# Half of a DFT's tables made on GpSimd instead of loaded, and another order of DMAs at the seam to the next stage

## The chip, the cores and the metric

One core of a Trainium2 chip runs the whole program. The metric is the device time in microseconds (us) of one execution; a lower one is better. The engines are TensorE (PE, with its weight loads PEld), VectorE (DVE), ScalarE (ACT), GpSimd (POOL) and SyncE (SP), and 16 DMA engines that all queues share. "SPq" and "ACTq" rows are DMA issues in the queues of SyncE and ScalarE.

## The reference, cut to what matters

A long convolution by FFT, gated by x, and behind it two dense layers:

```
h = (relu(pos_emb @ w1) @ w2) * exp(-0.01 * pos)      # 12480 x 128
u = x * v                                             # 2 x 12480 x 128
y = irfft(rfft(u, 2S) * rfft(h, 2S))[:S]
z = x * y
z = relu(z @ w_in)**2 @ w_out                         # 128 -> 2048 -> 128
z = (g * cos(g)) @ w_out2, g = z @ w_in2              # 128 -> 2048 -> 128
```

## The kernel before

The FFT is split as 104 x 120, and the program has three stages. **Stage 1** runs over 30 chunks q (`NCH`), each of two pairs i of sequence offsets (`CB`). `load(q)` brings one row block per chunk, `ld[q]`: 128 partitions x 2672 floats, holding x, v, a table `et` of cosines and sines (416 floats, `2 * KR`) and the position embedding. `mlp1` and `prep` make h (two matmuls, ACT) and u = x * v (GpSimd) in the tile `ut`; `pair(q, i)` multiplies u and h by the table on TensorE (`A`), ACT copies one half of the result to `v`, DVE writes sum and difference to the tile `bt`, and `store(q)` sends `bt` to the DRAM array `Bs`. The second pair of a chunk uses the same table with its halves swapped, and chunk 0 has one more table, in the tile `first` together with the small weights.

The chunks go through five load slots (`LDB`), so `load(q)` waits in SP's queue until PE is done with chunk q - 5. `prep` runs up to five pairs (`LA`) ahead of `pair`, and a tile `ut` comes free when `pair` of chunk q - 3 is done. Between pairs, `decode(2)` advances the unpacking of the 16 weight parts of the dense layers: seven steps to a part, so one part every 3.5 pairs, with five tensor_scalar (L101, L102, L104, L106, L109) and two two-input operations (L107, L112) on DVE and two (L114, L116) on GpSimd; L114 waits for L112's result. Each engine runs its instructions in the order in which the code is written (`manual_schedule`).

**Stage 2** multiplies along the other axis. `load2(g)` brings `B2[g]` from `Bs`, 26 groups of 8 rows, into the ring slots that chunks 25, 26 and 27 had; H, Z and d are its matmuls. At **the seam** the newest chunks are not yet in `Bs`. For chunks q >= `LATE` = 28 the first 32 rows (`KE`) go to a small DRAM array `Bx` by `store_late(q)` instead; `Bs` has zeros at their places; and `load_late(g)` then copies them into `B2[g]`, behind `load2(g)`. For group 0 the last chunk skips DRAM: four `direct` copies go from `bt` to `B2[0]`. `load2(0)` reads `Bs` and so waits for the landing of the store of chunk LATE - 1, which is issued at pair (LATE, 0). The stores of chunks 28 and 29 proper stand in SP's queue. **Stage 3**, the dense layers, takes the rest and isn't touched.

Of the kernel before, what the change touches and what calls it, by code (L numbers as in the profile page):

```python
# [8 lines left out]
F32 = mybir.dt.float32  # L9
# [4 lines left out]
ALU = mybir.AluOpType  # L14
# [23 lines left out]
LA = LDB = 5  # L38
NB = 3
BT = 3  # L40
LATE = NCH - 2
KE = 32
FIRST = 384 + 4 * NCH + 2 * KR
XVE, SLOT = 2048 + 2 * KR, 3072
CROSS = (1, 1)
WS = 59
INV2PI = 0.15915494309189535
# [9 lines left out]
def conv_moe(ctx, tc, t):  # L57
    nc = tc.nc
# [79 lines left out]

    def load_late(g, n=CB * (NCH - LATE)):

        for r in range(2):
            a = HB * r + CB * LATE
            nc.sync.dma_start(out=B2[g][a:a + n].rearrange("p k c e -> p k (c e)"),
                              in_=Bx[2 * G4 * g + r:2 * G4 * (g + 1):2, 0:n].rearrange("k p e -> p k e"))


    with ExitStack() as st:
        out1 = st.enter_context(tc.tile_pool(name="out1", bufs=BT))
        c1 = st.enter_context(tc.tile_pool(name="c1", bufs=1))
        ring1 = st.enter_context(tc.tile_pool(name="ring1", bufs=LDB - NB, side="right"))  # L150
        io = st.enter_context(tc.tile_pool(name="io1", bufs=2))
# [4 lines left out]
        first = c1.tile([128, FIRST], F32, name="first")  # L156
        w1b, w2b = first[:, 0:128], first[:, 128:384]
        win = first[0:N1, 384:384 + 4 * NCH].rearrange("p (q i a) -> p q i a", q=NCH, i=CB)
        emid = first[0:N1, 384 + 4 * NCH:FIRST].rearrange("p (a m) -> p a m", a=2)
        ld = {}  # L160

        def load(q):
            sl = slot("ld", *((ring, SLOT) if q % LDB < NB else (ring1, XVE + CB * N1)))
            nc.sync.dma_start(out=sl[:, 0:XVE + CB * N1], in_=t["ld"][q])
            x, v = (sl[0:N1, 1024 * n:1024 * (n + 1)].rearrange("p (i a d) -> p i a d", i=CB, a=2) for n in range(2))
            et = sl[0:N1, 2048:XVE].rearrange("p (a m) -> p a m", a=2)
            pt = sl[:, XVE:XVE + CB * N1].rearrange("p (i k) -> p i k", i=CB)
# [10 lines left out]
        def mlp1(q):  # L178
# [4 lines left out]
            nc.scalar.activation(hT, hp, AF.Relu)  # L183
            hT_t[q] = hT

        def prep(q, i):
            _, xt, vt, _ = ld[q]
            if i == 0:
                ut_t[q] = io.tile([N1, CB, 2, 384], F32, tag="ut", name="ut", bufs=3)
            u = ut_t[q]  # L190
            nc.gpsimd.tensor_tensor(out=u[:, i, :, 0:256], in0=xt[:, i], in1=vt[:, i], op=ALU.mult)
            hp = psM.tile([128, 2 * D], F32, tag="m", name="hp2")[0:N1].rearrange("p (a d) -> p a d", a=2)
            nc.tensor.matmul(hp, hT_t[q][:, i, :], w2b, start=True, stop=True)
            for a in range(2):
                nc.scalar.activation(u[:, i, a, 256:384], hp[:, a, :], AF.Copy, scale=win[:, q, i, a:a + 1])
# [24 lines left out]
        def store(q, eng=nc.scalar):  # L220
            a = KE if q >= LATE else 0
            put(eng, Bs[a:128, CB * q:CB * (q + 1)].rearrange("p x e -> p (x e)"), q, 0, a, 128)
            put(eng, Bs[128:KR, CB * q:CB * (q + 1)].rearrange("p x e -> p (x e)"), q, 1, 256 - KR, 128)

        def store_late(q):
            x = CB * (q - LATE)
            put(nc.scalar, Bx[:, x:x + CB].rearrange("p x e -> p (x e)"), q, 0, 0, KE)

        def direct(q, i, r, eng=nc.sync):

            p = HB * r + CB * q + i
            eng.dma_start(out=B2[0][p:p + 1].rearrange("p k c e -> p k (c e)"),
                          in_=bt_t[q][r:2 * G4:2, 0, i].rearrange("k c e -> k (c e)"))
# [11 lines left out]
        def last():  # L245
# [4 lines left out]
        upto("load", load, LDB, NCH)  # L250
        nc.sync.dma_start(out=Bs[0:KE, CB * LATE:HB].rearrange("p x e -> p (x e)"),
                          in_=bass.AP(t["ld"].tensor, 0, [[CB * (NCH - LATE) * 768, KE], [1, CB * (NCH - LATE) * 768]]))
        nc.scalar.dma_start(out=Gt, in_=t["G"])
        nc.scalar.dma_start(out=It, in_=t["IG"])
        for n, (q, i) in enumerate(seq):
            lead = min(LA, n + 1) if n else 1
            upto("mlp", mlp1, (n + lead - 1) // CB + 1, NCH)
            upto("prep", lambda m: prep(*seq[m]), n + lead, len(seq))
            pair(q, i, last if n == len(seq) - 1 else None)
            upto("mlp", mlp1, (n + lead + 1) // CB + 1 if n else 1, NCH)  # L260
            if i == 0 and q:
                if q > LATE:
                    store_late(q - 1)
                if q < NCH - 1:
                    store(q - 1)
            if (q, i) == (LATE, 0):
                load2(0)
                load2(1)
            if (q, i) == (NCH - 1, 0):
                load_late(0, CB * (NCH - 1 - LATE))  # L270
                direct(q, 0, 0)
                direct(q, 0, 1)
            if (q, i) == (NCH - 1, 1):
                load_late(1)
                load2(2)
                store(q - 1, nc.sync)
                store(q, nc.sync)
                load_late(2)
            if i == 1:
                upto("load", load, q + LDB + 1, NCH)  # L280
            if 1 < n < WS:
                decode(2)
# [428 lines left out]
def tables():  # L711
    import numpy as np
    s1, k1, s2 = np.arange(N1), np.arange(N1), np.arange(N2)
    b, kk = np.arange(HB), np.arange(HB)
    n = N2 * s1[:, None, None] + s2[None, :, None]
    th = 2 * np.pi * (((4 * k1[None, None, :] - 1) * n) % (4 * S)) / (4 * S)
    E = np.stack([np.cos(th), -np.sin(th)], 2)
    T = E.transpose(3, 1, 2, 0) / S
    E = E.reshape(N1, 2, HB, 2, N1).transpose(2, 0, 1, 4, 3).reshape(HB, N1, 2 * KR)
    G = np.zeros((2 * HB, 2, 128))  # L720
    I = np.zeros((128, 2, 2 * HB))
    for c in range(2):
        p = 2 * np.pi * ((2 * b[:, None] * kk[None, :] + b[:, None] * c) % N2) / N2
        C, Z = np.cos(p), np.sin(p)
        for n, o in enumerate(turns()):
            re, im = (HB + n, n) if n % CB and n > 1 else (n, HB + n)
            G[re, c, 0:60], G[im, c, 0:60] = C[o], Z[o]
            G[re, c, 64:124], G[im, c, 64:124] = -Z[o], C[o]
        I[0:60, c, 0::2], I[64:124, c, 0::2] = C.T, -Z.T
        I[0:60, c, 1::2], I[64:124, c, 1::2] = Z.T, C.T  # L730
    f = lambda a: np.ascontiguousarray(a, dtype=np.float32)
    win = np.exp(-0.01 * np.arange(S, dtype=np.float32))
    first = np.zeros((128, FIRST))
    first[0:N1, 384 + 4 * NCH:] = E[NCH]
# [18 lines left out]
def host(inp):  # L753
    import numpy as np
    c = np.ascontiguousarray
    out, T = tables()
    out["T"] = c(T.astype(np.float32).reshape(N1, N2 // CI, CI, 2, N1).transpose(1, 0, 2, 3, 4))
    a = inp["x"].reshape(2, N1, N2 // CI, CI, D)
    out["xT"] = c(a.transpose(2, 4, 3, 0, 1)).reshape(N2 // CI, D, CI, UT)
    for s, d in (("x", "xl"), ("v", "vl")):  # L760
        a = paired(inp[s].reshape(2, N1, 2, HB, D), 1, 3)
        out[d] = c(a.transpose(3, 1, 4, 2, 0, 5)).reshape(NCH, N1, 1024)
    xve = np.concatenate([out.pop("xl"), out.pop("vl"), out.pop("E")], 2)
    p = paired(inp["pos_emb"].reshape(N1, 2, HB, 64), 0, 2)
# [30 lines left out]
```

## Time and profile before

| | us |
|---|---|
| time before, median of 3 runs (2735.08 to 2741.74) | 2738.02 |
| the profiled execution's own time | 2745.54 |
| its span | 2743.4 |
| stage 1 with the seam, about | 0 to 243 |
| stage 2, about | 243 to 485 |
| stage 3 | 485 to the end |

The page gives PE 98% busy over the span; DVE and ACT 87% each, POOL 49%. Nine tenths of the span are stage 2 and 3, in which the DMA engines have little to do; in the first tenth they are full. A view over the whole span says nothing of the stretch that the change touches, so the rows below are of the first 265 us. Times within a view are microseconds from the span's start.

### The profile page before, as it was taken

The numbers are of one execution on the slowest core, as the hardware profiler recorded it, in microseconds if no ns is written. First come the engines' busy times: TensorE is split into PE (matmuls) and PEld (weight loads), VectorE is DVE, ScalarE is ACT, GpSimd is POOL, SyncE is SP. The second block draws the span as 40 slices with busy tenths as digits, with TensorE's granted clock in tenths as the row PEclk, the third lists the DMA queues.
The fourth block names the chain that finished last, engine by engine and source line by source line (L and its number), as shares of the span: only waits on it lengthen the run. The fifth ranks groups of instructions, "written<-read, shape, count | busy, mean of one in ns | idle before, by whom it ended". The sixth has DMA issues, their size and how long they took to land.

```text
span 2743.4 us, 38732 instructions
## 1 busy us (share of the span) xinstructions
PE 2689.5 (98%) x11740; PEld 2108.6 (77%) x11740; DVE 2390.2 (87%) x4675; ACT 2384.8 (87%) x4295; POOL 1352.9 (49%) x1050
## 2 busy tenths in 40 slices
PE   8987999999999999999999999999999999999999
PEld 5553444888888888888888888888888888888887
DVE  5886999788888888888888888888888888888888
ACT  4445998799999999999999999999999999999998
POOL 4554888144444444444444444444444444444445
PEclk9999999999999999999999999999999999999999
DMA  9997998210111110101110101110001111101000
GB/s 382 394 383 262 294 298 249 84 30 17 32 29 32 29 32 17 33 28 32 29 32 17 35 26 32 29 32 29 27 22 32 28 33 28 32 17 32 17 9 10
DMA packets 86771, 219.64 MB, mean 80 GB/s; under 512 B 6025, under 2 KB 49633, under 8 KB 82689
## 3 DMA queue, kind: packets, MB, share of 16 engines
q1 hardware_dynamic: 79298, 180.24, 20.4%
q10 hardware_dynamic: 7263, 36.92, 3.4%
q8 instruction: 93, 1.52, 0.2%
q14 instruction: 117, 0.96, 0.1%
HBM read 140.37 MB, written 77.07 MB: 79 GB/s over the span
## 4 chain that ended last, share of the span: by engine, by line
PE 80%; DVE 1%; ACT 1%; issue 0%; POOLq 0%; POOL 0%; DVEq 0%; ACTq 0%
PE h L555 13%; PE h L557 13%; PE y L571 13%; PE h L556 13%; PE y L569 13%; PE y L570 13%; PE pc L521 4%; DVE g L643 0%; DVE r L628 0%; ACT k L620 0%; DVE gh L653 0%; ACT c L635 0%; ACT g L600 0%; ACT r L594 0%; ACT gh L651 0%
## 5 line engine op out<-in xcount | busy, mean ns | idle before, releaser
L660 POOL TENSOR_TENSOR gl<-g,gh 128x512 fp32r<-128x512 f32 (+2 forms) x800 | 1041.7, 1302 | 1221.8 <-ACT gh L651 717.3
L643 DVE TENSOR_TENSOR g<-h,c 128x512 f32<-128x512 f32 (+2 forms) x800 | 538.4, 673 | 208.8 <-ACT c L635 196.8
L620 ACT ACTIVATE k<-h,quarter 128x512 int32<-128x512 f32 (+2 forms) x800 | 540.6, 676 | 121.5 <-PE h L557 117.1
L555 PE MATMUL h<-zh,wh 128*128 128x512 f32 (+2 forms) x1600 | 625.7, 391 | 1.1 <-DVE zh L539 0.8
L571 PE MATMUL y<-gl,wh 128*128 128x512 f32 (+2 forms) x1600 | 618.0, 386 | 4.2 <-POOL gl L660 2.4
L569 PE MATMUL y<-gh,wl 128*128 128x512 f32 (+2 forms) x1600 | 616.5, 385 | 0.1
L557 PE MATMUL h<-zh,wl 128*128 128x512 f32 (+2 forms) x1600 | 615.8, 385 | 0.0
L556 PE MATMUL h<-zl,wh 128*128 128x512 f32 (+2 forms) x1600 | 614.9, 384 | 0.0
L570 PE MATMUL y<-gh,wh 128*128 128x512 f32 (+2 forms) x1600 | 614.3, 384 | 0.0
L635 ACT ACTIVATE c<-r,halfpi 128x512 f32<-128x512 f32 (+2 forms) x800 | 565.3, 707 | 2.6 <-DVE r L628 2.6
L614 DVE TENSOR_TENSOR gl<-g,gh 128x512 fp32r<-128x512 f32 (+2 forms) x800 | 535.5, 669 | 1.1
L628 DVE CUSTOM_DVE_ANT_0 r<-h,k 128x512 f32<-128x512 f32 (+2 forms) x800 | 535.1, 669 | 0.0
L594 ACT ACTIVATE r<-h 128x512 f32<-128x512 f32 (+2 forms) x800 | 471.5, 589 | 70.2 <-PE h L557 59.0
L600 ACT ACTIVATE g<-r 128x512 f32<-128x512 f32 (+2 forms) x800 | 492.8, 616 | 1.0 <-DVE gl L614 0.4
L607 DVE CAST gh<-g 128x512 fp32r<-128x512 f32 (+2 forms) x800 | 331.4, 414 | 38.7 <-ACT g L600 35.6
L571 PEld LDWEIGHTS y<-gl,wh 128*128 128x128 f32 x1600 | 300.6, 188 | 70.4 <-POOL gl L660 7.7
L569 PEld LDWEIGHTS y<-gh,wl 128*128 128x128 f32 x1600 | 300.7, 188 | 60.6 <-DVE zl L582 1.2
L557 PEld LDWEIGHTS h<-zh,wl 128*128 128x128 f32 x1600 | 301.1, 188 | 59.9
L570 PEld LDWEIGHTS y<-gh,wh 128*128 128x128 f32 x1600 | 300.9, 188 | 59.5
L555 PEld LDWEIGHTS h<-zh,wh 128*128 128x128 f32 x1600 | 301.6, 189 | 56.7 <-issue 1.0
L556 PEld LDWEIGHTS h<-zl,wh 128*128 128x128 f32 x1600 | 301.4, 188 | 54.8
L651 ACT ACTIVATE gh<-g 128x512 fp32r<-128x512 f32 (+2 forms) x400 | 246.0, 615 | 0.1
(63 smaller groups left out, 2418.0 us busy)
## 6 DMA issues: line engine op xcount, KB each, us to landing
ld<-ld SPq DMA_DIRECT2D x30, 1336.0 KB
B<-Bs SPq DMA_DIRECT2D x25, 1536.0 KB
dt<-Ds SPq DMA_DIRECT2D x59, 416.0 KB
Ds<-dt SPq DMA_DIRECT2D x24, 960.0 KB
Bs<-bt ACTq DMA_DIRECT2D x28, 768.0 KB
Bs<-bt ACTq DMA_DIRECT2D x28, 480.0 KB
xt<-xT SPq DMA_DIRECT2D x60, 208.0 KB
out<-o SPq DMA_DIRECT2D x47, 256.0 KB
```

What stands on the lines that cost most here:

```text
L555: nc.tensor.matmul(h[:, :n], wh[:, f, :], zh[:, :n], start=True, stop=False)
L556: nc.tensor.matmul(h[:, :n], wh[:, f, :], zl[:, :n], start=False, stop=False)
L557: nc.tensor.matmul(h[:, :n], wl[:, f, :], zh[:, :n], start=False, stop=True)
L569: nc.tensor.matmul(y[:, :n], wl[:, f, :], gh[:, :n], start=a, stop=False)
L570: nc.tensor.matmul(y[:, :n], wh[:, f, :], gh[:, :n], start=False, stop=False)
L571: nc.tensor.matmul(y[:, :n], wh[:, f, :], gl[:, :n], start=False, stop=b)
L614: nc.vector.tensor_tensor(out=gl[:, :n], in0=g[:, :n], in1=gh[:, :n].bitcast(F32), op=ALU.subtract)
L620: nc.scalar.activation(k[:, :n], hp[2, u][:, :n], AF.Identity, scale=-1.0, bias=quarter)
L628: nc.vector._custom_dve(TENSOR_ADD_SAT, out=r[:, :n], in0=h[:, :n], in1=k[:, :n], s0=0.25, s1=-0.75)
L635: nc.scalar.activation(c[:, :n], r[:, :n], AF.Sin, bias=halfpi, scale=TWO_PI)
L643: nc.vector.tensor_tensor(out=g[:, :n], in0=h[:, :n], in1=c[:, :n], op=ALU.mult)
L660: nc.gpsimd.tensor_tensor(out=gl[:, :n], in0=g[:, :n], in1=gh[:, :n].bitcast(F32), op=ALU.subtract)
```

## The change

- Chunks with an odd q no longer load their table. `turn(q)` makes it from the table of chunk q - 1, by rotating each pair (cosine, sine) by one fixed angle per row: three GpSimd operations of 104 x 416 (old table with the pair's halves swapped x sine, into the tile `part`; old table x cosine; sum), written into the table's place in `ld[q]`. The cosines and sines (312 floats) lie behind the others in `first`. The table moves to the end of the row block, so that an odd chunk's load is 2256 floats and not 2672.
- `LATE` is 27, so three chunks are late instead of two: `Bx` has six columns, `store_late` runs for chunks 27, 28 and 29, and the zeros written to `Bs` grow by a half.
- `load2(0)` is issued at pair (27, 0), behind the store of chunk 26, and `load2(1)` at pair (28, 0).
- At the last two pairs the two `direct` copies of pair (29, 0) go ahead of `load_late(0)`, and `load_late(2)` goes ahead of the stores of chunks 28 and 29.

```diff
-LATE = NCH - 2
+LATE = NCH - 3
...
+            n = XVP if q % 2 else XVP + 2 * KR
+            nc.sync.dma_start(out=sl[:, 0:n], in_=t["ld"][q, :, 0:n])
...
+        def turn(q):
+            old, new = (ld[p][3].rearrange("p a (k r) -> p a k r", r=2) for p in (q - 1, q))
+            part = io.tile([N1, 2, N1, 2], F32, tag="part", name="part", bufs=1)
...
+            nc.gpsimd.tensor_tensor(out=part, in0=old[:, :, :, ::-1], in1=sine, op=ALU.mult)
+            nc.gpsimd.tensor_tensor(out=new, in0=old, in1=cosine, op=ALU.mult)
+            nc.gpsimd.tensor_tensor(out=new, in0=new, in1=part, op=ALU.add)
+
         def prep(q, i):
+            if i == 0 and q % 2:
+                turn(q)
...
-            if (q, i) == (LATE, 0):
-                load2(0)
-                load2(1)
+            if i == 0 and q in (LATE, LATE + 1):
+                load2(q - LATE)
             if (q, i) == (NCH - 1, 0):
-                load_late(0, CB * (NCH - 1 - LATE))
                 direct(q, 0, 0)
                 direct(q, 0, 1)
+                load_late(0, CB * (NCH - 1 - LATE))
             if (q, i) == (NCH - 1, 1):
                 load_late(1)
                 load2(2)
+                load_late(2)
                 store(q - 1, nc.sync)
                 store(q, nc.sync)
-                load_late(2)
```

GpSimd's queue in the middle of stage 1, before (w_b and wl belong to a weight part, ut to `prep`):

```order
L116 TENSOR_TENSOR wl10_68<-w_b_385,w_r_386 128x512
L191 TENSOR_TENSOR ut_435<-ld_333 104x2x256
L191 TENSOR_TENSOR ut_485<-ld_379 104x2x256 x2
L114 TENSOR_TENSOR w_b_463<-w_a_462,wh10_67 128x512
L191 TENSOR_TENSOR ut_531<-ld_430 104x2x256
L116 TENSOR_TENSOR wl10_68<-w_b_463,w_r_464 128x512
```

and the same place in the changed kernel, whose line numbers are up to 16 higher:

```order
L117 TENSOR_TENSOR wl10_68<-w_b_397,w_r_398 128x512
L204 TENSOR_TENSOR ut_451<-ld_345 104x2x256
L193 TENSOR_TENSOR part_501<-ld_345,first_102 104x416
L194 TENSOR_TENSOR ld_391<-ld_345,first_102 104x416
L195 TENSOR_TENSOR ld_391<-ld_391,part_501 104x416
L204 TENSOR_TENSOR ut_505<-ld_391 104x2x256 x2
L115 TENSOR_TENSOR w_b_479<-w_a_478,wh10_67 128x512
L204 TENSOR_TENSOR ut_551<-ld_446 104x2x256
L117 TENSOR_TENSOR wl10_68<-w_b_479,w_r_480 128x512
```

The three operations of `turn` stand between the last `ut` of the even chunk and the first of the odd one, ahead of the next w_b.

SP's queue at the seam, before (B2_1506, B2_1508 and B2_1561 are groups 0, 1 and 2; bt_1493 and bt_1526 are chunks 28 and 29):

```order
L136 DMA B2_1506<-Bs 128x4x768
L136 DMA B2_1508<-Bs 128x4x768
L143 DMA B2_1506<-Bx 2x4x768 x2
L232 DMA B2_1506<-bt_1526 1x4x768 x3
L143 DMA B2_1508<-Bx 4x4x768 x2
L136 DMA B2_1561<-Bs 128x4x768
L218 DMA Bs<-bt_1493 96x1536
L218 DMA Bs<-bt_1493 80x1536
L218 DMA Bs<-bt_1526 96x1536
L218 DMA Bs<-bt_1526 80x1536
L143 DMA B2_1561<-Bx 4x4x768 x2
```

and now (B2_1530, B2_1569 and B2_1622 are groups 0, 1 and 2; bt_1555 and bt_1587 are chunks 28 and 29):

```order
L137 DMA B2_1530<-Bs 128x4x768
L137 DMA B2_1569<-Bs 128x4x768
L245 DMA B2_1530<-bt_1587 1x4x768 x2
L144 DMA B2_1530<-Bx 4x4x768 x2
L245 DMA B2_1530<-bt_1587 1x4x768
L144 DMA B2_1569<-Bx 6x4x768 x2
L137 DMA B2_1622<-Bs 128x4x768
L144 DMA B2_1622<-Bx 6x4x768 x2
L231 DMA Bs<-bt_1555 96x1536
L231 DMA Bs<-bt_1555 80x1536
L231 DMA Bs<-bt_1587 96x1536
L231 DMA Bs<-bt_1587 80x1536
```

Two `direct` copies moved ahead of the late rows of group 0, and the late rows of group 2 ahead of the four stores; the late copies carry four and six partitions where they had two and four. The fourth `direct` copy is in ACT's queue in both.

## Rows read from the trace of the kernel before

**Rows 1.** Busy time by stretch: window, length, then engines, granted PE clock, DMA share, GB/s.
```profile
20.00:100.00 80.00, 75.12 (x251) 46.37 (x250) 65.93 (x86) 39.58 (x90) 39.33 (x31) 0.98 1.00 386
100.00:180.00 80.00, 71.97 (x223) 42.69 (x222) 66.92 (x82) 35.09 (x78) 42.74 (x33) 0.94 1.00 396
215.00:245.00 30.00, 20.25 (x60) 11.06 (x59) 18.59 (x29) 8.68 (x16) 7.59 (x6) 0.87 0.73 254
```
**Rows 2.** Timeline of PE: start, us; the first matmul of four chunks (mlp1).
```profile
38.94 0.52 PE L181 MATMUL hp<-ld,first 128*128 128x208 f32 x2
...
84.37 0.52 PE L181 MATMUL hp<-ld,first 128*128 128x208 f32 x2
...
90.75 0.52 PE L181 MATMUL hp<-ld,first 128*128 128x208 f32 x2
...
213.22 0.62 PE L181 MATMUL hp<-ld,first 128*128 128x208 f32 x2 [1.42 <-DMA ld<-ld]
```
**Rows 3.** PE's waits from 0 to 245 us: total, times, longest.
```profile
PE hp L181 <- DMA ld<-ld: 15.2, 10, 2.7
```
**Rows 4.** The page's DMA issues: count, KB each.
```profile
ld<-ld SPq DMA_DIRECT2D x30, 1336.0 KB
...
first<-first ACTq DMA_DIRECT2D x1, 460.0 KB
Bs<-ld SPq DMA_DIRECT2D x1, 384.0 KB
```
**Rows 5.** DVE by line, 0 to 245 us: busy us, mean ns, idle before.
```profile
L213 DVE TENSOR_TENSOR bt<-A,v 128x768 f32<-128x768 f32 x118 | 107.3, 950 | 47.7 <-PE A L209 43.6 <-ACT v L211 3.2 <-issue 0.5
L101 DVE TENSOR_SCALAR w_a<-wr 128x512 int32<-128x512 int32 x16 | 19.6, 1226 | 0.4 <-DMA wr<-moe_w_in 0.4
L102 DVE TENSOR_SCALAR w_b<-wr 128x512 int32<-128x512 int32 x16 | 17.3, 1084 | 0.0
L104 DVE TENSOR_SCALAR w_a<-w_a 128x512 f32<-128x512 f32 x16 | 11.1, 696 | 0.0
...
L112 DVE SCALAR_TENSOR_TENSOR w_r<-wr,w_b 128x512 f32<-128x512 uint32 x16 | 11.0, 686 | 0.3
L109 DVE TENSOR_SCALAR w_b<-w_a 128x512 int32<-128x512 int32 x16 | 6.8, 422 | 0.3
```
**Rows 6.** GpSimd by line, same stretch.
```profile
L191 POOL TENSOR_TENSOR ut<-ld 104x512 f32<-104x512 f32 x60 | 78.4, 1324 | 39.2 <-PE A L209 29.5 <-DMA ld<-ld 9.7
L114 POOL TENSOR_TENSOR w_b<-w_a,wh 128x512 f32<-128x512 f32 x16 | 20.4, 1274 | 75.9 <-DVE w_r L112 67.1 <-ACT v L211 8.8
```
**Rows 7.** Timeline of DVE where GpSimd is busy without a gap.
```profile
187.47 1.49 DVE L102 TENSOR_SCALAR w_b<-wr 128x512 int32<-128x512 int32 x1
```
**Rows 8.** Timeline at the seam, all engines.
```profile
218.82 0.81 ACTq L218 DMA_DIRECT2D Bs<-bt  x2
...
224.85 0.81 ACTq L218 DMA_DIRECT2D Bs<-bt  x2
...
228.95 1.26 SPq L136 DMA_DIRECT2D B<-Bs  x2
...
231.32 2.75 DVE L213 TENSOR_TENSOR bt<-A,v 128x768 f32<-128x768 f32 x4
...
236.68 0.59 SPq L143 DMA_DIRECT2D B<-Bx  x2
237.36 1.98 SPq L232 DMA_DIRECT2D B<-bt  x3
...
243.42 3.75 PE L313 MATMUL H<-B,Gt 120*128 120x512 f32 x4 [8.39 <-DMA B<-bt]
...
243.94 3.27 SPq L218 DMA_DIRECT2D Bs<-bt  x4
...
252.60 1.03 SPq L143 DMA_DIRECT2D B<-Bx  x2
...
260.59 1.45 PE L313 MATMUL H<-B,Gt 120*128 120x512 f32 x2 [3.00 <-DMA B<-Bx]
```

More of the change, by code (lines that the diff above doesn't have):

```diff
@@ L40 @@
 BT = 3
-LATE = NCH - 2
+LATE = NCH - 3
 KE = 32
-FIRST = 384 + 4 * NCH + 2 * KR
-XVE, SLOT = 2048 + 2 * KR, 3072
+TURN = 384 + 4 * NCH + 2 * KR
+FIRST = TURN + N1 + KR
+XVP, SLOT = 2048 + CB * N1, 3072
 CROSS = (1, 1)
@@ L158, in conv_moe @@
         win = first[0:N1, 384:384 + 4 * NCH].rearrange("p (q i a) -> p q i a", q=NCH, i=CB)
-        emid = first[0:N1, 384 + 4 * NCH:FIRST].rearrange("p (a m) -> p a m", a=2)
+        emid = first[0:N1, 384 + 4 * NCH:TURN].rearrange("p (a m) -> p a m", a=2)
         ld = {}
         def load(q):
-            sl = slot("ld", *((ring, SLOT) if q % LDB < NB else (ring1, XVE + CB * N1)))
-            nc.sync.dma_start(out=sl[:, 0:XVE + CB * N1], in_=t["ld"][q])
+            sl = slot("ld", *((ring, SLOT) if q % LDB < NB else (ring1, XVP + 2 * KR)))
+            n = XVP if q % 2 else XVP + 2 * KR
+            nc.sync.dma_start(out=sl[:, 0:n], in_=t["ld"][q, :, 0:n])
             x, v = (sl[0:N1, 1024 * n:1024 * (n + 1)].rearrange("p (i a d) -> p i a d", i=CB, a=2) for n in range(2))
-            et = sl[0:N1, 2048:XVE].rearrange("p (a m) -> p a m", a=2)
-            pt = sl[:, XVE:XVE + CB * N1].rearrange("p (i k) -> p i k", i=CB)
+            et = sl[0:N1, XVP:XVP + 2 * KR].rearrange("p (a m) -> p a m", a=2)
+            pt = sl[:, 2048:XVP].rearrange("p (i k) -> p i k", i=CB)
             ld[q] = (pt, x, v, et)
@@ L184, in mlp1 @@
             hT_t[q] = hT
+        def turn(q):
+            old, new = (ld[p][3].rearrange("p a (k r) -> p a k r", r=2) for p in (q - 1, q))
+            part = io.tile([N1, 2, N1, 2], F32, tag="part", name="part", bufs=1)
+            cosine = first[0:N1, TURN:TURN + N1].unsqueeze(1).unsqueeze(3).to_broadcast([N1, 2, N1, 2])
+            sine = first[0:N1, TURN + N1:FIRST].rearrange("p (k r) -> p k r", r=2).unsqueeze(1).to_broadcast([N1, 2, N1, 2])
+            nc.gpsimd.tensor_tensor(out=part, in0=old[:, :, :, ::-1], in1=sine, op=ALU.mult)
+            nc.gpsimd.tensor_tensor(out=new, in0=old, in1=cosine, op=ALU.mult)
+            nc.gpsimd.tensor_tensor(out=new, in0=new, in1=part, op=ALU.add)
         def prep(q, i):
+            if i == 0 and q % 2:
+                turn(q)
             _, xt, vt, _ = ld[q]
@@ L733, in tables @@
     first = np.zeros((128, FIRST))
-    first[0:N1, 384 + 4 * NCH:] = E[NCH]
+    first[0:N1, 384 + 4 * NCH:TURN] = E[NCH]
+    ph = 2 * np.pi * (4 * k1 - 1) / (4 * S)
+    first[0:N1, TURN:TURN + N1] = np.cos(ph)
+    first[0:N1, TURN + N1:] = np.stack([np.sin(ph), -np.sin(ph)], 1).reshape(KR)
     win = paired(win.reshape(N1, 2, HB), 0, 2).transpose(0, 2, 3, 1)
@@ L762, in host @@
         out[d] = c(a.transpose(3, 1, 4, 2, 0, 5)).reshape(NCH, N1, 1024)
-    xve = np.concatenate([out.pop("xl"), out.pop("vl"), out.pop("E")], 2)
+    xv = np.concatenate([out.pop("xl"), out.pop("vl")], 2)
     p = paired(inp["pos_emb"].reshape(N1, 2, HB, 64), 0, 2)
     pos = c(p.transpose(2, 1, 4, 3, 0)).reshape(NCH, 128, CB * N1)
-    out["ld"] = np.concatenate([np.pad(xve, [(0, 0), (0, 128 - N1), (0, 0)]), pos], 2)
+    xv, e = (np.pad(b, [(0, 0), (0, 128 - N1), (0, 0)]) for b in (xv, out.pop("E")))
+    out["ld"] = np.concatenate([xv, pos, e], 2)
     for a in range(2):
```

## Prediction

> **What bounds the kernel now.** I read the busy time by stretch first, since the whole-span shares are those of the dense layers. In [rows 1] the DMA share is 1.00 from 20 to 180 us, at 386 and 396 GB/s (mean 391), while PE is busy 75 and 72 of 80 us, DVE 66 and 67, GpSimd 39 and 43. So stage 1 goes at the pace of the DMA engines. Two checks. The first matmul of a chunk comes 23 chunks apart at 38.94 and 213.22 us [rows 2], 7.58 us per chunk; a chunk on which PE waits for nothing takes 6.38 us (84.37 to 90.75, in the same group). And what PE waits for is loads: 15.2 us in 10 waits [rows 3]. PE has over a microsecond of room per chunk. DVE has less. A weight part comes every 3.5 pairs, 1.75 chunks or 13.26 us. In that time DVE does 3.5 x 107.3/59 = 6.37 us of `bt`, five tensor_scalar at 1.23, 1.08, 0.70, 0.42 and 0.42 us and two two-input operations at 0.69 [rows 5] (L106 and L107, not among them, read as L109 and L112 do): 6.37 + 3.85 + 1.38 = 11.6 us, 87%.
>
> The seam I read from the timeline [rows 8]. `load2(0)` is issued at 228.95, 4.1 us behind the issue of chunk 27's store at 224.85, and its late rows follow only at 236.68, when it has landed. The `direct` copies stand behind those (237.36, done 239.34), and the first matmul of stage 2 starts at 243.42 after 8.39 us of idle PE. The data for them was there earlier: DVE had the first half of the last pair at 231.32 + 2.75 = 234.07. A second wait follows: group 2's late rows are issued at 252.60, behind four stores (243.94) that hold 2.2 MB (96 and 80 partitions x 1536 floats, twice), and H at 260.59 has waited 3.00 us for them.
>
> **The change, part by part.**
>
> *Bytes.* 15 loads lose 416 floats x 128 partitions = 208 KB each of the 1336 [rows 4]: 3.195 MB. `first` grows from 460 KB by 312 x 128 floats, 0.160 MB, and the zeros from 384 KB by half, 0.197 MB. Net 2.84 MB less ahead of the last load's landing; at 391 GB/s that is **7.3 us**, or 0.24 per chunk, from 7.58 to 7.34. It is on the path as long as the DMA engines stay the slowest. Stores, weight loads and PE's work are as before, and PE at 6.38 is no limit.
>
> *GpSimd's new work.* Three operations of 416 columns per odd chunk. No row has an operand with swapped neighbours or a repeated one; the nearest is L114's 1.274 us for 512 columns [rows 6], which gives 1.04 us each, 3.1 per odd chunk and 47 us in all. I take that; the other end is half that speed, 2.1 us each and 94 in all (an estimate: twice the row). GpSimd's busy share goes from 51% to about 73%. For its own consumers there is room: it has waited 29.5 us for PE to free `ut` and 67.1 us for L112 [rows 6], the three operations need only a table that has landed, and `ut` is made four pairs (some 15 us) ahead of its use. Queued behind them are `ut` of the odd chunk and the next w_b; both still come early.
>
> *What that does to DVE.* L101, L102 and L104 take 1.23, 1.08 and 0.70 us on average, L109 0.42, with 512 columns each [rows 5]. The long ones are those that meet a running GpSimd operation: L102 takes 1.49 us in a stretch where GpSimd has no gap [rows 7], about one GpSimd operation (1.27) more than 0.42 would be long. L101 and L102 come within a few us of L112, when GpSimd runs its train w_b, wl, ut, ut; L106 and L109 come when it waits for L112. With 3.1 us more in the train, L104 falls under it, and L106 and L109 sometimes. I put L104 at L102's 1.08 and the other two halfway there, 0.75: five then cost 1.23 + 1.08 + 1.08 + 0.75 + 0.75 = 4.89, and DVE's part takes 6.37 + 4.89 + 1.38 = 12.64 us against 1.75 x 7.34 = 12.84 for the DMA engines. Two engines so close don't overlap without loss. I take half of the DMA gain as lost, 3.6 us (ends: nothing lost, and the rival below). **Stage 1: -3.7 us.**
>
> The Trainium skill (SBUF — State Buffer, section SBUF: two separate sides) states that VectorE in its two-port modes and GpSimd share a port pair as an exclusive lock, held for a whole instruction, and the other blocks. That speaks against this change; the row of 1.49 us agrees, and taken to its end the rule is the third rival.
>
> *The seam, group 0.* `load2(0)` now waits for chunk 26's store, issued at 218.82 in old time [rows 8]. With the same 4.1 us that gives 222.9, and with the same 7.7 us for itself (228.95 to 236.68) 230.6; chunk 27's store now shares its time, so I say 232. That is ahead of 234.07, so the last pair's data is late next. A `direct` copy issued then, 0.66 us (1.98/3), and on the way as long as the last one before (239.34 to 243.42, 4.1 us) lets H start at 238.9: **-4.5 us**. Nearest end: 2 us on the way instead of 4.1 (an estimate, half the row, since less of `load2(1)` stands ahead), -6.6. Far end: `load2(0)` and chunk 27's store delay each other until nothing is won, 0. ACT's `direct` no longer holds up ACT's queue, and with it the last half of `v`. The late rows of group 0 are now 4 partitions per copy and not 2, and sit between the `direct` copies: 0.6 us of issue, in the same wait.
>
> *The seam, group 2.* Its late rows no longer follow the stores, so H's 3.00 us go: **-3.0** (ends 0 and -3). The four stores move behind them by about the load of group 2; group 3's load is queued behind the stores, and its slot comes free no earlier than the stores' issue ends, so I cost it at nothing; uncovered it would take back up to the same 3.0. PE's granted clock averages 0.87 from 215 to 245 [rows 1], so about a quarter of that at 1.2 GHz and not 2.4, behind idle time; a shorter gap may give 1.5 us more, which I leave to the range.
>
> *Sum.* -3.7 - 4.5 - 3.0 = -11.2. The profiled execution took 2745.54 us, 7.5 above the median of 2738.02; taking the difference over: 2734.3 by its own time, **2727** by the median.
>
> **The rivals.**
>
> 1. *Nothing is lost to DVE, and the copies come at the near end.* The five tensor_scalar stay at 3.85 us: -7.3 - 6.6 - 3.0 = -16.9, 2721. For it: GpSimd's idle time before `ut` is where the operations may fall, away from DVE's. Against: their place in the queue, right behind w_b and wl.
> 2. *The seam doesn't come earlier.* `load2(0)` and `load2(1)`, 3.1 MB, now run against chunk 27's store, and group 3 takes the 3.0 us back. Only -3.7 is left: 2734. For it: the DMA share is still 0.73 there [rows 1]. Against: that is not full.
> 3. *The lock decides, and the kernel is slower.* If all five tensor_scalar meet a running GpSimd operation, each takes the 1.49 us of [rows 7]: 5 x 1.49 + 1.38 + 6.37 = 15.2 us per weight part against 13.26 now, +1.9 x 16 = +31 us in stage 1; with -7.5 at the seam +23.5: 2761. It decides from the point where DVE's part takes 13.26 + 7.5/16 = 13.7 us, a mean tensor_scalar of 1.19 us (0.77 now, 0.98 in my sum). Operations at the 2.1 us end push there too, since GpSimd would then be busy some 95% of the stage.
> 4. *The lock in part.* DVE's part takes about 13.7 us: stage 1 loses what the seam wins, 2738.
>
> **How the numbers follow.** Forecast 0.52, rival 1 0.16, rival 2 0.13, rival 3 0.09, rival 4 0.10. The bound for "same" is 0.2%, 5.5 us (about what a measurement of this kernel can tell from no change): 2732.5 to 2743.5. Faster: most of the forecast (0.50), rival 1, and a little of rival 2 (0.04): 0.70. Same: the rest of the forecast (0.02), most of rival 2 (0.09), most of rival 4 (0.09): 0.20. Slower: rival 3 and a little of rival 4: 0.10. The range takes in rivals 1, 2 and 4 with their bounds, and leaves out rival 3 and the outer edges: 2716 to 2739.
>
> **What the profile after would show.** Bytes: the first matmuls of chunks 7.3 to 7.5 us apart, and the DMA share still near 1.0; a share near 0.95 means that DVE or GpSimd sets the pace. Lock: L104, L106 and L109 longer than 0.70, 0.42 and 0.42 us; if they are unchanged my loss of 3.6 was too much. `turn`: three operations near 1.04 us. Seam: 8.39 us of idle before H become about 4, and the wait of 3.00 us on group 2's late rows is gone, with none on group 3's. The prediction is wrong if GpSimd's operations take twice as long, if DVE's tensor_scalar average over 1.19 us, or if H of groups 0 to 3 waits as long as before.

## Result, and the profile after

The changed kernel takes 2759.24 us (median of 6 runs, 2755.43 to 2761.29) against 2740.28 (2735.08 to 2748.41) of the kernel before on the same chip: a ratio of 1.0064, 95% interval 1.0052 to 1.0076. It is slower by 19 us, where 2727 was forecast; the time is that of the third rival. The profiled execution took 2757.65 us, its span 2755.9.

Busy time by stretch of the kernel after, columns as in [rows 1]:

```profile
20.00:100.00 80.00, 73.28 (x237) 44.28 (x236) 68.22 (x77) 37.03 (x84) 56.35 (x46) 0.96 0.98 362
100.00:180.00 80.00, 68.35 (x228) 40.87 (x227) 73.06 (x83) 34.50 (x78) 56.95 (x46) 1.00 0.97 356
```

GpSimd went from 39 and 43 us to 56 and 57, VectorE from 66 and 67 to 68 and 73. The DMA engines moved 386 and 396 GB/s and now 362 and 356, although their share still reads 0.98 and 0.97: a share near one doesn't say that they set the pace. The last chunk's first matmul comes at 221.56 us and not 213.22 [rows 2]. PE's waits from 0 to 300 us (total, times, longest), to compare with [rows 3]:

```profile
PE A L222 <- DVE bt L226: 19.3, 16, 3.2
PE hp L183 <- DMA first<-first: 8.3, 1, 8.3
PE H L325 <- DMA B<-bt: 6.7, 1, 6.7
PE H L325 <- DMA B<-Bx: 4.6, 1, 4.6
...
PE hp L183 <- DMA ld<-ld: 1.2, 2, 0.8
```

Loads cost PE 15.2 us before and 1.2 now; VectorE's `bt` costs it 19.3. So stage 1 is no longer bound by the loads but by VectorE. Where VectorE's time went, by line from 0 to 275 us (as in [rows 5]; L102, L103, L105, L107 and L108 were L101, L102, L104, L106 and L107):

```profile
L226 DVE TENSOR_TENSOR bt<-A,v 128x768 f32<-128x768 f32 x118 | 107.1, 948 | 35.6 <-PE A L222 27.1 <-ACT v L224 5.1 <-issue 3.4
L102 DVE TENSOR_SCALAR w_a<-wr 128x512 int32<-128x512 int32 x16 | 23.7, 1483 | 0.0
L103 DVE TENSOR_SCALAR w_b<-wr 128x512 int32<-128x512 int32 x16 | 20.1, 1256 | 4.5 <-POOL wl L117 4.5
L108 DVE TENSOR_TENSOR w_a<-w_a,w_b 128x512 int32<-128x512 int32 x16 | 17.4, 1089 | 0.6
L105 DVE TENSOR_SCALAR w_a<-w_a 128x512 f32<-128x512 f32 x16 | 15.0, 939 | 0.0
L107 DVE TENSOR_SCALAR w_a<-w_a 128x512 int32<-128x512 int32 x16 | 12.6, 789 | 0.3
L113 DVE SCALAR_TENSOR_TENSOR w_r<-wr,w_b 128x512 f32<-128x512 uint32 x16 | 11.0, 687 | 0.3
```

and, for the two-input operation L108, the same line before (0 to 245 us):

```profile
L107 DVE TENSOR_TENSOR w_a<-w_a,w_b 128x512 int32<-128x512 int32 x16 | 11.1, 692 | 0.6
```

`bt`, which reads PSUM, is as it was. The unpacking took 83.6 us before (all seven lines added) and takes 106.5 now. The three operations of `turn` on GpSimd:

```profile
L193 POOL TENSOR_TENSOR part<-ld,first 104x416 f32<-104x416 f32 x15 | 16.8, 1120 | 0.0
L195 POOL TENSOR_TENSOR ld<-ld,part 104x416 f32<-104x416 f32 x15 | 16.5, 1102 | 1.2
L194 POOL TENSOR_TENSOR ld<-ld,first 104x416 f32<-104x416 f32 x15 | 16.2, 1080 | 0.0
```

How the 23 us arise is seen in single operations. Timeline of the kernel after (start, length), GpSimd and VectorE:

```profile
158.35 1.66 DVE L108 TENSOR_TENSOR w_a<-w_a,w_b 128x512 int32<-128x512 int32 x1
...
164.18 1.29 POOL L204 TENSOR_TENSOR ut<-ld 104x512 f32<-104x512 f32 x1
164.44 2.54 DVE L102 TENSOR_SCALAR w_a<-wr 128x512 int32<-128x512 int32 x1
...
165.44 1.26 POOL L117 TENSOR_TENSOR wl<-w_b,w_r 128x512 fp32r<-128x512 f32 x1
...
166.66 1.24 POOL L193 TENSOR_TENSOR part<-ld,first 104x416 f32<-104x416 f32 x1
166.91 1.29 DVE L103 TENSOR_SCALAR w_b<-wr 128x512 int32<-128x512 int32 x1
...
167.87 1.16 POOL L194 TENSOR_TENSOR ld<-ld,first 104x416 f32<-104x416 f32 x1
```

L103 starts while L193 runs; L193 ends at 167.90, L103 at 168.20. L102 starts under `ut` and ends at 166.98, 0.28 us behind L117's end at 166.70: it lost the place to a second GpSimd operation. This is not one picked case. I call it a **meeting** when an operation of the unpacking is longer than it is alone (0.42 us, 0.69 with two inputs) by over 0.05. The trace before has 28 meetings among 112 operations, the trace after 56, and every one of the 84 ends 0.28 to 0.29 us, with two inputs 0.55 us, behind the end of a GpSimd operation. The other way round, 86 operations of the two traces start while a GpSimd operation runs; 84 of them are these, and the other two start in its last 0.14 us. So VectorE waits for the end of that GpSimd operation, on average for 0.9 to 1.0 us per meeting. L110 and L113 never meet one: GpSimd then waits for L113's result.

That is what the Trainium skill (SBUF — State Buffer, section SBUF: two separate sides) states of the port pair, for VectorE in a two-port mode: an exclusive lock, which the second one to come waits for. The trace agrees in all 84 cases, though no view names the mode that the tensor_scalar run in. The same section of the Trainium skill names VectorE operations with two SBUF inputs as well, against a GpSimd operation that reads SBUF. The rise of L108 from 0.69 to 1.09 us agrees.

The seam after (SyncE's queue and H, as in [rows 8]):

```profile
246.79 1.41 SPq L245 DMA_DIRECT2D B<-bt  x2
...
251.04 0.63 SPq L144 DMA_DIRECT2D B<-Bx  x2
251.76 0.59 SPq L245 DMA_DIRECT2D B<-bt  x1
...
255.32 3.75 PE L325 MATMUL H<-B,Gt 120*128 120x512 f32 x4 [6.67 <-DMA B<-bt]
...
261.05 0.60 SPq L144 DMA_DIRECT2D B<-Bx  x2
261.71 4.43 SPq L231 DMA_DIRECT2D Bs<-bt  x4
...
266.24 2.02 SPq L137 DMA_DIRECT2D B<-Bs  x1
...
277.74 0.62 SPq L144 DMA_DIRECT2D B<-Bx  x2
...
282.68 1.33 PE L325 MATMUL H<-B,Gt 120*128 120x512 f32 x2 [4.61 <-DMA B<-Bx]
```

The wait of group 2 [rows 8] is gone, and group 3 has one of 4.61 us.

### The profile page after: what moved, and what is told of

Its sections match the earlier page's. It is cut to its first block, busy times and chain, and to the rows that moved or that the text cites. A ratio compares the mean times of both kernels' runs of the same rounds, so it can differ in the third digit from the quotient of the medians.

```text
span 2755.9 us, 38778 instructions
## 1 busy us (share of the span) xinstructions
PE 2691.3 (98%) x11740; PEld 2107.9 (76%) x11740; DVE 2412.8 (88%) x4675; ACT 2382.5 (86%) x4295; POOL 1404.3 (51%) x1095
## 4 chain that ended last, share of the span: by engine, by line
PE 80%; DVE 1%; ACT 1%; issue 0%; DMA 0%; POOL 0%; SPq 0%; DVEq 0%; ACTq 0%
PE h L567 13%; PE h L569 13%; PE y L583 13%; PE y L581 13%; PE h L568 13%; PE y L582 13%; PE pc L533 4%; DVE r L640 0%; DVE g L655 0%; ACT k L632 0%; DVE gh L665 0%; ACT r L606 0%; ACT g L612 0%; ACT c L647 0%; ACT gh L663 0%
```

## Experiments

Theories: **L**, GpSimd's additional operations hold up VectorE's unpacking; **S**, the new seam costs; **B**, the bytes or their layout; **P**, GpSimd's own products come late; later **V** (VectorE's time by the meetings, which is L made exact), **Q** (ScalarE's queue stands ahead of `wh`), **T** (the length of GpSimd's train), **C** (the early loads collide with chunk 27's store), **G** (group 3 behind the stores), **H** (each turn costs its share), **W** (the work costs wherever VectorE's operations stand), **U** (held-up `bt`).

### The two halves apart

`e1_turn_only` is the kernel after with the old seam, `e2_seam_only` the kernel before with the new one.

> The changed kernel with its seam undone (LATE 28, the old order of DMAs), so the turned tables and shorter loads alone. Theory L (GpSimd's new operations hold up VectorE's weight unpacking, and stage 1 goes at VectorE's pace): as slow as the changed kernel or a little slower, 14 to 24 us above the kernel before; the first matmuls of chunks 7.8 to 7.9 us apart; PE waits for bt on VectorE and not for loads. Rival S (the seam's new order costs the time): faster than before by 3 to 8 us, the saved bytes.

> The kernel before with the seam of the changed one alone; all tables are loaded. Theory L: stage 1 as before (7.58 us per chunk), and 3 to 8 us faster in all, since the 8.39 us of idle time before the first H become 4 to 7 and the 3.00 us before group 2 go. Rival S: 10 to 20 us slower.

2754.41 and 2746.91 against 2741.96: ratios 1.0048 (1.0033 to 1.0063) and 1.0021 (1.0011 to 1.0030). Both halves lose, +12.5 and +5.0 us, and their sum is near the whole. For e1 this is L's side, a little under its 14 to 24, with the chunks 7.86 us apart. For e2 neither theory has it: L wanted 3 to 8 us faster, S 10 to 20 slower, and the idle time before the first H stays at 8.43 us.

### The bytes without the work, the work without the bytes

`e3_bytes_only` (from e1):

```diff
-            if i == 0 and q % 2:
-                turn(q)
...
+            if q % 2:
+                return emid[:, a if i == 0 else 1 - a]
```

`e4_work_only` (from e1):

```diff
-            n = XVP if q % 2 else XVP + 2 * KR
+            n = XVP + 2 * KR
...
-            old, new = (...)
+            old = ld[q - 1][3].rearrange("p a (k r) -> p a k r", r=2)
+            new = io.tile([N1, 2, N1, 2], F32, tag="spare", name="spare", bufs=1)
```

> As the run with the turned tables alone, but the three GpSimd operations are left out: odd chunks multiply by the one extra table in the tile first instead of a turned one, so odd chunks' results are those of another table. Theory L: the bytes then count, 4 to 8 us faster than before, chunks 7.3 to 7.4 us apart. Rival B (the shorter loads or the new layout cost time by themselves): not faster.

> All tables are loaded as before, and GpSimd does its three operations all the same, into a tile that nobody reads; old seam. Theory L: as slow as the turned tables alone, or slower by what the bytes still gave: 14 to 28 us above before, with VectorE's tensor_scalar at 0.9 us and more on average. Rival B: no slower than before.

e3: 2734.85, 0.9980 (0.9968 to 0.9992); e4: 2753.65, 1.0050 (1.0032 to 1.0068). The bytes give what the forecast priced at 7.3 (-7.1); the chunks come 7.10 us apart in the profiled execution, under the 7.3 to 7.4 expected. B falls with it. The work alone (+11.7, under L's 14 to 28) costs as much as e1 does, though nobody reads its result and no byte is saved; so it isn't the turned table that comes late. P, GpSimd's own products, stays open here, since they stand behind the same work in e4. e3 also prices the work where loads are short: e1 - e3 = 19.6 us, while the unpacking differs by 107.3 - 90.1 = 17.2. In e3 VectorE is busy 76.55 of 80 us in the second stretch and the loads still run at 399 GB/s:

```profile
20.00:100.00 80.00, 76.64 (x260) 47.12 (x259) 68.77 (x87) 41.61 (x94) 41.39 (x33) 1.00 0.99 392
100.00:180.00 80.00, 73.46 (x238) 43.75 (x237) 76.55 (x88) 36.87 (x83) 47.26 (x36) 0.98 1.01 399
```

PE's wait for `bt` in e3 from 0 to 300 us:

```profile
PE A L222 <- DVE bt L226: 3.0, 4, 1.4
```

So VectorE's share of busy time isn't what decides: it is 145 of the 160 us here, where the bytes are won, and 141 in the kernel after, where VectorE holds PE up for 19.3 us and not 3.0.

### Taking VectorE's operations out

`e7_turn_light` is e1, `e8_before_light` the kernel before, each without five of the seven operations of a weight part (a sixth then reads another tile):

```diff
-        ts(out=b, in0=hi, scalar1=-0x80000000, scalar2=0x40000000, ...)
-        ts(out=af, in0=af, scalar1=2.0 ** -15, scalar2=122880.0, ...)
-        ts(out=a, in0=a, scalar1=4, scalar2=1, ...)
-        nc.vector.tensor_tensor(out=a, in0=a, in1=b, op=ALU.bitwise_xor)
-        ts(out=b, in0=a, scalar1=-0x800000, scalar2=None, ...)
...
-        nc.vector.scalar_tensor_tensor(out=rf, in0=lo, scalar=2.0 ** -52, in1=bf, ...)
+        nc.vector.scalar_tensor_tensor(out=rf, in0=lo, scalar=2.0 ** -52, in1=af, ...)
```

> The turned tables alone (old seam), with VectorE's weight unpacking cut down: L102, L104, L106, L107 and L109 of the kernel before are left out, so the dense weights are other numbers; one tensor_scalar and one two-input operation stay per weight part, GpSimd's and ScalarE's parts too. Theory L (VectorE held up in the unpacking): the turned tables then cost nothing, and this is 4 to 8 us faster than the same cut in the kernel before; chunks 7.1 to 7.4 us apart. Rival P (GpSimd's own products come too late for TensorE): still slower than the same cut in the kernel before, by 5 us or more.

> The kernel before with the same cut in the weight unpacking (the same five operations left out, so other weights), as the partner of the run above. Both theories: stage 1 stays at the pace of the loads, 7.5 to 7.6 us per chunk, so the time is that of the kernel before within 4 us.

2736.39, 0.9980 (0.9969 to 0.9990), and 2741.19, 0.9997 (0.9984 to 1.0010). With VectorE relieved, turning is worth -5 us: the loss of e1 is gone and PE waits for loads again (e7, PE's waits from 0 to 300 us):

```profile
PE hp L178 <- DMA ld<-ld: 13.7, 11, 3.1
```

So P, which wanted e7 slower than e8 by 5 us or more, falls. This run takes the victim away together with its own work, so by itself it doesn't show that the meetings are the cause and not just VectorE's load. But it shows that GpSimd's added work costs nothing where it brings hardly any meetings: of the 32 operations left, 20 meet GpSimd in e7 and 19 in e8, and the unpacking takes 30.9 and 29.6 us.

### Where the work stands

`e9_turn_wh_late` (from e1) moves ScalarE's copy `wh` one step later; `e10_turn_spread` puts the three operations of `turn` behind three different `ut`:

```diff
-        nc.scalar.activation(wh[:, f], af, AF.Copy)
         nc.vector.scalar_tensor_tensor(...)
         yield
+        nc.scalar.activation(wh[:, f], af, AF.Copy)
```

```diff
+            if q % 2 == 0:
+                turn(q + 1, i)
+            elif i == 0:
+                turn(q, 2)
```

> The turned tables alone (old seam), with ScalarE's copy wh of a weight part moved one step later in the unpacking, next to the GpSimd operation that reads it. Theory Q (ScalarE stands in its queue before wh, 46 us in the changed kernel, and holds up ut and v behind it): that wait falls to below 15 us, and 5 to 12 of the 13 us that the turned tables cost come back. Rival V (VectorE's own time is the limit): within 3 us of the turned tables alone.

> The turned tables alone (old seam), with GpSimd's three operations apart: the first and the second behind the products of the even chunk's two pairs, the third behind the first product of the odd chunk. Theory T (it is the long unbroken train on GpSimd that catches L104 to L107): the mean of these falls, and 3 to 8 us come back. Rival V (as many operations meet VectorE wherever they stand): within 3 us of the turned tables alone.

2754.32, 1.0051 (1.0034 to 1.0067), and 2757.92, 1.0057 (1.0037 to 1.0077). Neither gives anything back, and e10 (+16.2) is even 3.7 us above e1, past V's bound of 3. In e9 ScalarE's wait ahead of `wh` shrinks from 49.4 to 19.2 us (for L108; below 15 was Q's condition), but the meetings rise from 57 to 64. So Q is not priced by itself here; what is seen is that PE's wait for `bt` went up, from 21.3 to 26.5, while ScalarE waited 30 us less; what ScalarE may have given back went into more meetings. T falls: spread, the train has 56 meetings, as many as in one piece.

`e11_turn_half` (from e1) turns the tables of chunks 1, 5, 9, ... only; `e12_half_early` is the same with the early loads of e6 (below).

```diff
-            if i == 0 and q % 2:
+            if i == 0 and q % 4 == 1:
                 turn(q)
```

> Only chunks 1, 5, 9, ... have their table turned by GpSimd (7 of the 15 at most, with 7 or 8 loads shorter); the other odd chunks load it whole; the old seam. Theory V (VectorE's time: the turn lengthens VectorE's unpacking by about 1.4 us per weight part, and stage 1 is slower only as far as that passes the loads' pace): half the turns lengthen it by about 0.7 us, to about 13.1 us per part by the pace of 7.89 us x 1.75 = 13.8 at the full dose, which is the loads' own pace of 7.46 x 1.75 = 13.06; so the time is within 4 us of the kernel before, 2738 to 2745 beside 2741. Rival H (each turn costs its share, whatever the pace): half of the full dose's +12.8, so 2747 to 2748. Rival F (few trains fit into VectorE's slack and the bytes are won): -2 to -4, 2737 to 2739.

> The same half of the turns, with LATE 27, the early load2(0) and load2(1) and the direct copies ahead of load_late(0), but load_late(2) behind the stores of the last two chunks as in the kernel before. Since the early loads alone gave -1 us and load_late(2) ahead of the stores was what cost the seam its gain, V expects e11's time within 3 us, 2737 to 2744, and in the trace a wait of group 2 of under 3 us and none of 4 or more at group 3. Rival H: 2746 to 2748. Rival C (load2(0) against chunk 27's store costs in the seam): 3 to 5 above e11.

2745.50, 1.0023 (1.0013 to 1.0033), and 2746.57, 1.0025 (1.0014 to 1.0037), against 2740.69. F falls: half the bytes, worth some 3.5 us by e3, are gone and 5 us more. V's "within 4 us" and H's half share (+6 to +7) both miss e11's +4.8 by about a microsecond, and its interval (+3.6 to +9.0) holds both, so these two aren't told apart. Meetings go from 28 to 44 with 8 turns, and PE waits 7.5 us for loads in 7 waits and 10.0 for `bt` in 9: the two limits seem to take turns, so that VectorE's slack in one part doesn't pay for a train in another. Its mean share of 87% was not room for these trains. e12's 2746.57 is in H's range (2746 to 2748) and above V's (2737 to 2744). In e12 group 2 waits 3.61 us, over the 3 I had set as a bound, and group 3 not at all; the seam is too small to be read from its total.

### Taking only the meetings away

All work stays; VectorE's seven operations of a part stand behind every 3.5th pair in one run (`e13_turn_bunch7`, `e15_before_bunch7`) or in two, four and three (`e14_turn_bunch43`, `e16_before_bunch43`), where GpSimd has run out of other work. e13 and e14 are from e1, e15 and e16 from the kernel before.

```diff
-            if 1 < n < WS:
-                decode(2)
+            if n == 2:
+                decode(1)
+            if n > 1 and n in [2 + 7 * k // 2 for k in range(16)]:
+                decode(7)
```

> All the turns, the old seam, nothing left out; the seven VectorE operations of a weight part stand in one run behind every 3.5th pair, where GpSimd, out of other work, waits for their result, instead of two steps behind each pair. Theory V (a VectorE operation of the unpacking that meets a running GpSimd operation waits for its end, some 0.9 us each, and 57 of 112 meet one): no more than 16 to 20 meet one, the unpacking takes 70 to 76 us and not 107, and the loads set the pace again: about 7.3 us per chunk, 2733 to 2738, if PE's room takes a stretch of 3.5 us without bt. Rival W (GpSimd's additional 50 us of work cost the same wherever VectorE's operations stand, through the table coming late or through SBUF in general): 2752 to 2756 with the unpacking above 95 us. Rival U (the meetings go, but a run of 3.5 us on VectorE holds up bt and so PE): unpacking 70 to 76 us and yet 2745 to 2755, with PE's waits for bt above 15 us.

> The same in two runs behind two neighbouring pairs, four operations and three, with one pair's bt between. V: 16 to 24 meetings, unpacking 72 to 80 us, 2733 to 2739; PE's waits for bt smaller than in one run of seven. W: 2752 to 2756. U: between this and one run of seven the one with less wait for bt is the faster.

> The kernel before (all tables loaded, no turn, old seam) with the unpacking in one run of seven per part. V: fewer than 10 meetings beside 28, unpacking near 60 us beside 83.6; as the loads set the pace, the time is that of before within 3 us, 2738 to 2744. U: 2743 to 2750 by held-up bt. W says nothing of it.

> The kernel before with the unpacking in two runs (four operations and three) behind neighbouring pairs. V: unpacking 60 to 66 us, the time of before within 3 us, 2738 to 2744. With e14: by V the difference e14 minus this is -4 to -7 (the bytes alone), by W +12.

Against 2740.97: e13 2766.51, 1.0096 (1.0067 to 1.0124); e14 2763.24, 1.0082 (1.0054 to 1.0109); e15 2764.92, 1.0093 (1.0067 to 1.0119); e16 2751.31, 1.0040 (1.0026 to 1.0054). In time no theory came out. V had e13 and e14 at 2733 to 2739 and the other two within 3 us of before, W had the first two at 2752 to 2756, and U's ranges (e13 2745 to 2755, e15 2743 to 2750) are too low. The meetings went in e13, e15 and e16 (13, 0 and 3), and these were slower than the kernels that they come from all the same, which is U's direction; in e14 45 stayed, where V wanted 16 to 24. VectorE and PE in e13, by line from 0 to 275 us and PE's waits from 0 to 300:

```profile
L103 DVE TENSOR_SCALAR w_b<-wr 128x512 int32<-128x512 int32 x16 | 12.1, 757 | 0.0
...
L108 DVE TENSOR_TENSOR w_a<-w_a,w_b 128x512 int32<-128x512 int32 x16 | 11.1, 693 | 0.5
```

```profile
PE hp L206 <- DVE w_r L113: 14.9, 7, 3.6
PE A L222 <- ACT v L224: 10.3, 7, 2.1
```

The unpacking is nearly back at the length that it has alone (63.6 us in all; 56.0 in e15, where nothing meets), and PE now waits for the last of the run of seven, by the trace's naming, and for ScalarE; `bt` itself is 0.8 us of it, where U wanted over 15. ScalarE stands ahead of `wh` for 63.1 us (49.4 in e1). What the four were to tell is the price of the added work at equal placement. From e15 to e13 it brings 13 meetings, and the last chunk's first matmul moves from 227.68 to 228.47 us; from e16 to e14 it brings 42, and that matmul moves from 218.02 to 229.64, the median by +11.9. W wanted +12 in both, and by what was expected the second pair is W's (V: -4 to -7). But V's figure was for a placement with few meetings, which e14 isn't, so this pair fits both and tells nothing. The medians of the first pair differ by only 1.6, but with 4 runs each over 9 to 12 us that alone would not exclude much; and since both are bound elsewhere, added work could also hide there. What speaks against W is e7 beside e8: about as many meetings, and the added work costs nothing. So V rests on the trace of single operations, on e4 beside e3, and on e7 beside e8, with e13 against e15 in agreement.

| kernel | meetings of 112 | unpacking, us | median less before, us |
|---|---|---|---|
| before | 28 | 83.6 | 0 |
| e3 bytes only | 32 | 90.1 | -7.1 |
| e11 half the turns | 44 | 96.0 | +4.8 |
| e4 work only | 56 | 106.5 | +11.7 |
| e1 turn only | 57 | 107.3 | +12.5 |
| e10 spread | 56 | 105.8 | +16.2 |
| e9 `wh` later | 64 | 113.8 | +12.6 |
| e16, e15 before, bunched | 3, 0 | 57.5, 56.0 | +10.3, +24.0 |
| e14, e13 turn, bunched | 45, 13 | 95.4, 63.6 | +22.3, +25.5 |

The length of the unpacking doesn't order the times by itself: e9 has 6.5 us more of it than e1 at the same time, e10 1.5 us less at 3.7 us more. What one meeting costs the kernel, beyond VectorE's own 0.9 us, depends on what stands behind it, and no run prices that.

### The seam

`e5_late2_first` is the kernel before with one line moved; `e6_early_loads` is e2 with that line moved back.

```diff
                 load2(2)
+                load_late(2)
                 store(q - 1, nc.sync)
                 store(q, nc.sync)
-                load_late(2)
```

> The kernel before, but with group 2's late rows ahead of the four stores in SP's queue, and nothing else of the new seam. Theory G (the new place of the stores delays group 3's load behind them, which the seam alone showed as a wait of 5.28 us): the 3.00 us before group 2's H go, 3 to 6 us appear before group 3's, and the time is 0 to 4 us above before. Rival: 3 us faster, group 3 in time.

> The kernel before with three late chunks, the earlier loads of groups 0 and 1 and the direct copies ahead of group 0's late rows; group 2's late rows stay behind the stores. Theory C (the earlier loads share the DMA engines with chunk 27's store, and chunk 28's rows in Bx land behind both, so that group 0 is complete no sooner): 30 to 32 us from the last chunk's first matmul to the first H, as against 30.2 before, a wait of 2 to 4 us before group 2, none before group 3; 0 to 3 us above before. Rival: the first H 3 us or more sooner, and as much faster.

e5: 2744.48, 1.0009 (0.9995 to 1.0023); e6: 2741.41, 0.9997 (0.9986 to 1.0009), against 2742.71. e6 is the new seam without the moved line, and nothing remains of e2's +5. SyncE's queue in e2, then in e6:

```profile
254.12 0.60 SPq L143 DMA_DIRECT2D B<-Bx  x2
...
254.78 4.72 SPq L218 DMA_DIRECT2D Bs<-bt  x4
...
259.60 1.84 SPq L136 DMA_DIRECT2D B<-Bs  x1
...
270.92 0.62 SPq L143 DMA_DIRECT2D B<-Bx  x2
...
276.16 2.04 PE L312 MATMUL H<-B,Gt 120*128 120x512 f32 x2 [5.28 <-DMA B<-Bx]
```

```profile
227.56 1.33 SPq L136 DMA_DIRECT2D B<-Bs  x2
237.87 1.39 SPq L232 DMA_DIRECT2D B<-bt  x2
242.87 0.63 SPq L143 DMA_DIRECT2D B<-Bx  x2
243.59 0.59 SPq L232 DMA_DIRECT2D B<-bt  x1
...
245.58 1.99 SPq L218 DMA_DIRECT2D Bs<-bt  x4
247.20 3.75 PE L312 MATMUL H<-B,Gt 120*128 120x512 f32 x4 [7.46 <-DMA B<-bt]
...
253.59 2.03 SPq L143 DMA_DIRECT2D B<-Bx  x2
...
256.58 0.76 SPq L136 DMA_DIRECT2D B<-Bs  x1
262.02 1.10 PE L312 MATMUL H<-B,Gt 120*128 120x512 f32 x2 [0.65 <-DMA B<-Bx]
...
266.10 0.60 SPq L143 DMA_DIRECT2D B<-Bx  x2
```

`load_late(2)` waits for group 2's load to land. Moved ahead, it holds the four stores, which wait for nothing, from 245.58 to 254.78; group 3's load behind them goes 3 us later, runs against their 2.2 MB, and its late rows leave at 270.92 and not 266.10. From the first H to that of group 3 it is 28.2 us in e2, 23.8 in e6, 27.5 before and 29.7 in e5. G is right, though group 3's wait in e5, 2.92 us, is just under its 3 to 6; e5 alone (+1.8, interval over zero) is too small to show it in the total, where e2 against e6 (some 6 us) does.

C is right too, as far as group 0 goes: the early loads win nothing for the first H. Its wait of 2 to 4 us before group 2 was 0.65, and the time is 1.3 us below before and not 0 to 3 above. In e6 `load2(0)` is issued 11.3 us behind the last chunk's first matmul (216.24; before 15.7, [rows 2, 8]) but the `direct` copies that wait for it leave 10.3 us after its issue, where it was 7.7; H comes 31.0 us behind that matmul, 30.2 before. Chunk 27's store (576 and 480 KB, issued at 229.92) now runs beside it, and `load_late(0)` leaves only at 242.87, with the last `direct` copy behind it. The trace puts that last wait down to a landing from `Bs` (3.6 us) and not, as C had it, to chunk 28's rows in `Bx` (0.2 us).

## Why the prediction was wrong

- *What bounds the kernel*: right, and shown by e3 (-7.1 from the bytes alone). But VectorE at 87% was taken to have room for the trains at the price of half the gain; in e11 half of them already cost more than their bytes win.
- *Bytes, -7.3*: right in size (e3 -7.1, e7 -5).
- *`turn`, 1.04 us each*: 1.08 to 1.12, 49.5 us in all. The end of 2.1 us is out.
- *VectorE, 12.64 us per weight part, half of the DMA gain lost*: **the step that failed**. The five tensor_scalar came out as summed (4.89; single ones not: L102 1.48 for 1.23, L110 0.42 for 0.75). Missing was L108 (L107 in the kernel before): two-input operations were put at their old 0.69 us without a reason, and it grew by 0.40 us. That makes 13.02, some 0.4 more. As much again is the loss beside VectorE's own time: I took the pace to be 0.4 us above it (13.06), and by 7.89 us per chunk in the kernel after it is 13.81, 0.8 above. That loss doesn't follow from two engines being close, as the prediction has it: in e3 VectorE's part took 6.37 + 90.1/16 = 12.0 us beside chunks 7.10 us apart, 12.4 per part, and the bytes came out whole. How the delays of single operations add up to it is not shown. The 0.75 us between 13.06 and 13.81, times 16 parts, are 12 of the 16 us by which stage 1 missed (-3.7 forecast, +12.5 in e1). The other four come behind it: PE's first matmul of the last chunk runs ahead of `bt`, and from it to the first H it is 34.4 us in e1, 30.2 before.
- *Seam, group 0, -4.5*: wrong; the far end, 0, is what e6 shows (-1.3, interval over zero). The step (4.1 and 7.7 us as before, 1.4 us more for chunk 27's store) undersized the sharing (the copies leave 21.6 us behind the last chunk's first matmul in e6, where 18.8 was forecast), and "0.6 us of issue" for the late rows missed that they wait and hold the last `direct` copy (27.4 us behind it, where 20.9 was forecast).
- *Seam, group 2, -3.0, group 3 at nothing*: the 3.00 us went, as said, and the uncovered end came: 4.61 us at group 3 (5.28 in e2). The 3.00 were themselves one execution's: e1, with the old seam, has 1.03 us at group 2 and 1.83 at group 3. The prediction named the load queued behind the stores, and not that the stores themselves are now queued behind a wait. For both seam steps the sum was -7.5; it is +5.0 in e2 and, as a difference of medians, some +6.5 between e1 and the kernel after.
- *Rivals*: the third has the mechanism and the time (2761), with other terms: it had every tensor_scalar meet GpSimd and the seam gain 7.5. Half of the operations do, and the seam loses. That its time fits is luck: its stage 1 was 18.5 us too slow (+31 for +12.5) and its seam 14 too fast. Its threshold, a mean tensor_scalar of 1.19 us, was wrong: the mean is 0.98 and the kernel is slower by 19, since the threshold left out both L108 and the loss beside VectorE's own time. Its chance of 0.09 rested on that threshold.

Left open: what Q costs by itself, how the single delays add up to the lost time, and whether any placement has neither the meetings nor the waits of the bunched runs. No version tried that computes the whole beats the kernel before.

## What to carry to other kernels

Before you give work to GpSimd, count how many of VectorE's SBUF operations will start while it runs: here each such meeting cost the rest of a GpSimd operation, about 0.9 us, and 49.5 us of work on a GpSimd that was half idle brought 28 more of them. Mean slack doesn't say whether a train of work fits between two engines that both run in order: VectorE held the kernel up at 88% busy (after) and didn't at 91% (e3). Ask what each operation of the train will delay. And a DMA issue that waits, moved ahead of ones that don't, moves those too: look at what stands behind it in its queue, and at who reads next.

## What the runs showed that I had not expected

- A VectorE operation that meets GpSimd ends a constant time behind it, 0.28 us (0.55 with two inputs), in 84 of 84 cases, though it takes 0.42 (0.69) alone; it can lose a second time to the next GpSimd operation (2.54 us for one of 0.42). The wait goes both ways: in the kernel after, `ut` on GpSimd takes 1.29 us on average where it starts with no unpacking operation running, and 1.53 us in the 30 of 60 cases where one runs.
- `bt`, two inputs with one in PSUM, is untouched: 950 and 948 ns.
- The DMA share stays at 0.97 while the rate falls from 391 to 359 GB/s.
- The swapped or repeated operand costs GpSimd nothing to speak of: 1.12 and 1.08 us against 1.10 for the plain sum of the same size.
